# Gated mix of a spectral filter and a lookup of experts: last slices loaded once, one table along d, merged twiddle tables, one more late row buffer

## The chip, the core and the metric

The kernel runs on one core of one Trainium2 chip. The metric is the device time in microseconds (us) of one execution; several executions give a median. A profile is one further execution, recorded by the hardware profiler. Engines are called PE (matmuls), DVE (vector), ACT (scalar), POOL and SP (here used to issue transfers).

## The reference

x has 2048 rows (s) of 576 columns (d). Two results are mixed row by row with a gate.

```python
def A(x, w_r, w_i):                      # spectral filter
    X = rfft2(x, axes=(-2, -1)) * (w_r + 1j * w_i)
    return irfft2(X, s=(2048, 576), axes=(-2, -1))

def B(x, w_q, k1, k2, u, v):             # 32 heads, 64 x 64 experts, the best one
    q = einsum("nd,dhc->nhc", x, w_q)    # c: 2 x 128
    i1 = argmax(q[..., :128] @ k1.T); i2 = argmax(q[..., 128:] @ k2.T)
    e = i1 * 64 + i2                     # one row of u and of v per head
    g = softmax over the single best     # = 1
    return einsum("nhk,nhk,nhkd->nd", g, gelu(einsum("nd,nhkd->nhk", x, u[e])), v[e])

g = sigmoid((x * gate_w).sum(-1))
out = g * A + (1 - g) * B
```

## The kernel before

The 2048 rows are 16 tiles of 128. A small planner (`Plan`) holds the whole program: each helper (`dv`, `ac`, `ld`, `plan`) records a job with its engine, an assumed duration, a due time `at` and its buffers, which come from rings of a given size. `Plan.order` then lists the jobs by their due times, as their inputs and free buffers allow, and the loop at the end of `tile_kernel` writes each engine's instructions out in this order, chained so that no engine departs from it. The due times of the parts of A are multiples of the constant `FPACE`. A ring whose name is in `plan.late` opens only when the last job on a buffer of the score stage has ended; at that point (`switch`) the pools of the score stage are closed and new ones open in their place.

**Score stage.** The products of w_q and the keys are formed for one chunk of four heads at a time (`build_m`, 8 chunks): the 576 columns are cut into five slices i of 128, the last of which holds only 64, and carried twice. `load_wq` (L352) brings 512 KB for each chunk and slice on SP; 8 matmuls with the keys kT make 512 columns in PSUM; ACT (L396) copies these as the rounded high part `mh`, DVE (L397) subtracts it to get the low part `ml`. x comes transposed in blocks of 512 rows (`load_x`, L358): ACT (L361) makes its high part, DVE (L362) its low part. `scores` multiplies x and the products in high and low parts: three matmuls for each of the slices 0 to 3 (hi x hi, hi x lo, lo x hi) and two for the last slice, in which both copies of the 64 columns are used so that one matmul does two of these products. DVE takes the maximum of each 64 (L427), ACT the sign of the difference (L435), and a few small steps on ACT and DVE (L446 to L455) give the index. With mh and ml in rings of 8, chunk c+1 is built while chunk c is scored.

**Groups.** A group is a tile and a chunk, four heads. POOL issues a gather (L487) of 128 rows of u and v, joined to 1152 columns, into a buffer of the ring `uv` (12) or, late, `uv2`. DVE forms the product with x and sums it (L496), ACT the gelu (L500), DVE the factors a (L501). Then either DVE adds the four rows of v (L512, L514), or, for about half of the groups of tiles 10 to 15 and some others (`is_d`), ACT makes four diagonal matrices (L524) and PE multiplies with them (16 passes), and the PSUM result is copied or added (L538, L540). Groups of the tiles 0 to 9 run during the score stage, those of tiles 10 to 15 after it.

**The transform.** After the score stage `fold` splits each tile into sums and differences along d (DVE L649 to L651, ACT L648), multiplies with kr (five matmuls, PE) and ACT (L661, L662) spreads the result in `BT`. Then ten units follow: `f2` (six matmuls with the table `fi[0]`), `f4` (four matmuls with the twiddle table `t4`), `f5` (DVE L709 to L712, complex product with w), `f6` (matmuls with the table `t6`) and copies and sums back in `BT` (ACT L766, DVE L775 to L782). `turns` loads t4 and t6 for a unit on SP (L680, L681) and ACT (L682 to L684) makes the negated and doubled columns. After the last unit, `invert` takes each tile back: six matmuls with the table `fi[1]`, ACT L819, four matmuls with krb, ACT L830 and L831 with the gate as scale. `mix` (DVE L835) adds the part of B and stores the tile (SP). The kr table, the late tiles of x (L366), `fi[0]` (L638), the gate row (L639), `fi[1]` (L640) and krb (L641) are loaded by SP, in the written-out order; an SP load that waits for its buffer holds up those behind it.

The matmuls have one line, L313, that of the helper `mm`.

Of the kernel before, what the change touches and what calls it, by code (L numbers as in the profile page):

```python
# [19 lines left out]
P = 128  # L20
D = 576
# [11 lines left out]
def _tables():  # L33
# [19 lines left out]
    fwd = np.stack([  # L53
        rows(np.cos, np.arange(0, 128)), rows(np.cos, np.arange(128, 256)), ct,
        -rows(np.sin, np.arange(0, 128)), -rows(np.sin, np.arange(128, 256)), -st,
    ])
    ck = np.full(DF, 2.0)
    ck[0] = ck[-1] = 1.0
    ck /= S * D

    def irows(fn, ks):
        return fn(2 * np.pi * np.outer(ks, k) / D) * ck[ks][:, None]

    ct = z.copy()
    ct[:33] = irows(np.cos, np.arange(256, 289))
    st = z.copy()
    st[64:96] = irows(np.sin, np.arange(256, 288))
    inv = np.stack([
        irows(np.cos, np.arange(0, 128)), irows(np.cos, np.arange(128, 256)), ct,
        irows(np.sin, np.arange(0, 128)), irows(np.sin, np.arange(128, 256)), st,  # L70
# [12 lines left out]
        "t_fi": c(np.concatenate([fwd, inv]).transpose(1, 0, 2)),  # L83
        "t_f4": c(f4),
        "t_f6": c(f6),
# [167 lines left out]
def tile_kernel(ctx, tc, xn, xT, wqT, kT, wri, uv, gw, t_kr, t_fi, t_f4, t_f6, t_io, out):  # L253
# [84 lines left out]
    gate = pp.tile([P, NT], F32, tag="gate", name="gate")  # L338
    gone = pp.tile([P, NT], F32, tag="gone", name="gone")
# [12 lines left out]
    def load_wq(c, i, at, after=()):  # L352
        w = wq_t[c, i] = buf("uv", ROW, view=lambda x: x.rearrange("p a d -> p (a d)")[:, : 8 * P].rearrange("p (g e) -> p g e", g=8))
        ld(load(P * 4096, 4096), at, lambda: nc.sync.dma_start(w.ap, wqT[c, i]), [w], after=after)

    def load_x(b, i, at, at2):
        st = buf("uv", ROW, view=lambda x: x[:, 0, :512])
        ld(load(P * 2048, 2048), at, lambda: nc.sync.dma_start(st.ap, xT[:, i, b * 512 : b * 512 + 512]), [st])  # L358
        hi = xts[i if i < 4 else 8][b]
        lo, r = (xts[4 + i][b], 0) if i < 4 else (hi, 64)  # L360
        ac(act(512), at2, lambda: actv(hi.ap, st.ap, AF.Copy), [hi], [st])  # L361
        dv(dve(512), at2, lambda: vt(lo.ap[r:], st.ap[r:], hi.ap[r:].bitcast(F32), ALU.subtract), [lo], [st, hi])  # L362
# [18 lines left out]
    def build_m(c, i, at, after=()):  # L381
        mh, ml = m_t[c, i] = [buf(n, [P, CW], F32R) for n in ("mh", "ml")]
        pm = psum()
        wq = wq_t[c, i]
        pv = lambda: pm.ap.rearrange("p a (g e) -> p (a g) e", e=128)

        def go():
            for g in range(8):
                half = g % 2
                mm(  # L390
                    pv()[:, g, :], wq.ap[:, g, :],
                    kTb.ap[:, half * 64 : half * 64 + 128], start=True, stop=True)
# [3 lines left out]
        ac(act(512), at, lambda: actv(v3(mh), pv()[:, :, :E], AF.Copy), [mh], [pm])  # L396
        dv(dve(512, True), at, lambda: vt(v3(ml), pv()[:, :, :E], v3(mh).bitcast(F32), ALU.subtract), [ml], [pm, mh])  # L397
# [4 lines left out]
    def scores(c, tp, at):  # L402
# [4 lines left out]
        def part(j, i):  # L407
# [5 lines left out]
            seq = [(x, mh), (x, ml)] + ([(xts[4 + i][b], mh)] if i < 4 else [])  # L413

            def go():
                for n, (xx, m) in enumerate(seq):
                    mm(ps.ap[:, j, :], xx.ap[:, tsl], m.ap, start=i == n == 0, stop=i == 4 and n == len(seq) - 1)

            use = {id(q): q for pair in seq for q in pair}
            return plan("PE", 0.23 * len(seq), at, go, [(ps, j)], list(use.values()))  # L420
# [211 lines left out]
    fi = [buf("fi0", [P, 6, DF]), buf("fi1", [P, 6, DF])]  # L632
# [5 lines left out]
    ld(load(P * 6936, 4096), T0 + 8, lambda: nc.sync.dma_start(fi[0].ap, t_fi[:, 0:6, :]), [fi[0]])  # L638
    ld(0.5, T0 + 15, lambda: nc.sync.dma_start(gw2.ap, gw.partition_broadcast(P)), [gw2])  # L639
    ld(load(P * 6936, 4096), T0 + 90, lambda: nc.sync.dma_start(fi[1].ap, t_fi[:, 6:12, :]), [fi[1]])  # L640
# [4 lines left out]
    def fold(t, at):  # L645
        x = xs[t]
        f = buf("f5", [P, ND * P])
        ac(0.17, at, lambda: actv(f.ap[:, 0:385:384], x.ap[:, 0:1].to_broadcast([P, 2]), AF.Copy), [(f, 0)], [x])  # L648
# [28 lines left out]
    def turns(k, at):  # L677
        t4 = buf("t4", [P, 3, P])
        t6 = buf("t6", [P, 5, P])
        ld(load(P * 1024, 1024), at - 8, lambda: nc.sync.dma_start(t4.ap[:, 0:2, :], t_f4[k]), [(t4, 0)])  # L680
        ld(load(P * 1024, 1024), at - 8, lambda: nc.sync.dma_start(t6.ap[:, 0:2, :], t_f6[k]), [(t6, 0)])  # L681
        ac(act(128), at - 2, lambda: actv(t4.ap[:, 2, :], t4.ap[:, 1, :], AF.Copy, scale=-1.0), [(t4, 1)], [(t4, 0)])  # L682
        ac(act(256), at - 2, lambda: actv(t6.ap[:, 2:5:2, :], t6.ap[:, 0:1, :].to_broadcast([P, 2, P]), AF.Copy), [(t6, 1)], [(t6, 0)])
        ac(act(128), at - 2, lambda: actv(t6.ap[:, 3, :], t6.ap[:, 1, :], AF.Copy, scale=-1.0), [(t6, 2)], [(t6, 0)])  # L684
        tabs[k] = t4, t6

    def f4(k2, X, at):
# [16 lines left out]
        return p, w, t6

    def f5(p, w, t6, at):
# [4 lines left out]
        dv(dve(DF), at, lambda: vt(a.ap[:, 0, :], a.ap[:, 0, :], b.ap[:, 1, :], ALU.subtract), [(a, 0)], [b])  # L711
        dv(dve(DF), at, lambda: vt(a.ap[:, 1, :], a.ap[:, 1, :], b.ap[:, 0, :], ALU.add), [(a, 1)], [b])  # L712
        return a, t6

    def f6(k2, zb, t6, at):
        pt = psum()
        u, v = (0, 3) if k2 <= 8 else (2, 1)

        def go():
            z, T = zb.ap, t6.ap  # L720
# [9 lines left out]
        plan("PE", 4 * pe(256) + 4 * pe(128), at, go, [pt], [(zb, 0), (zb, 1), (t6, 0), (t6, 1), (t6, 2)])  # L730
# [10 lines left out]
    def unit_front(k2, at):  # L741
# [8 lines left out]
        ac(act(DF), at, lambda: actv(sr.ap[:, 0, :], psn.ap[:, 1, :DF], AF.Copy, scale=-1.0), [(sr, 0), sr], [psn])  # L750
        ac(act(DF), at, lambda: actv(sr.ap[:, 1, :], psn.ap[:, 0, :DF], AF.Copy), [(sr, 1), sr], [psn])
# [4 lines left out]
    def unit_back(z, at):  # L756
# [19 lines left out]
        dv(dve(256, True), at, lambda: vt(tslot(qs, 0), tm()[:, 1], mainv(pb)[:, 1], ALU.subtract), [(BT, "q", qs, 0)], src + [s_])  # L776
        dv(dve(256, True), at, lambda: vt(tslot(qs, 1), mainv(pb)[:, 0], tm()[:, 0], ALU.subtract), [(BT, "q", qs, 1)], src + [s_])
# [3 lines left out]
        dv(dve(128, True), at, lambda: vt(BT.ap[0:33, 2, :, qs], ta.ap[64:97, 512:], pb.ap[64:97, 1, :P], ALU.subtract), [s_], src)  # L781
        dv(dve(128, True), at, lambda: vt(BT.ap[64:96, 2, :, qs], pb.ap[0:32, 1, :P], ta.ap[0:32, 512:], ALU.subtract), [s_], src)  # L782
# [13 lines left out]
    def close_gates(at):  # L796
# [7 lines left out]
        dv(0.1, at, lambda: nc.vector.tensor_scalar(gone, gate, -1.0, 1.0, op0=ALU.mult, op1=ALU.add), ["gone"], ["gate"])  # L804

    gas = {}

    def invert(t, at):
        p = psum()

        def go():
            for r in range(2):
                for m, i in enumerate((3 * r, 3 * r + 1, 2)):
                    mm(p.ap[:, r, :DF], BT.ap[:, i, t * 8 : t * 8 + 8, :].rearrange("p j q -> p (j q)"),
                       fi[1].ap[:, 3 * r + m, :], start=m == 0, stop=m == 2)

        plan("PE", 6 * pe(DF), at, go, [p], [fi[1]] + every)
# [11 lines left out]
        g = gate[:, t : t + 1]  # L829
        ac(act(DF), at + 3, lambda: actv(ga.ap[:, :DF], p9.ap[:, 0, :DF], AF.Copy, scale=g), [(ga, 0)], [p9, "gate"])  # L830
        ac(act(DF), at + 3, lambda: actv(ga.ap[:, 575:288:-1], p9.ap[:, 1, 1:288], AF.Copy, scale=g), [(ga, 1)], [p9, "gate"])  # L831
# [98 lines left out]
```

## Time and profile before

| | before |
|---|---|
| median of 3 runs | 1009.44 us (1008.35 to 1010.46) |
| the profiled execution | 1001.24 us |
| span in its profile | 999.5 us |
| mean granted PE clock | 0.965 |
| PE busy | 904.4 us (90%) |
| DVE busy | 916.7 us (92%) |
| ACT busy | 514.6 us (51%) |
| POOL busy | 574.4 us (57%) |
| moved | 348.39 MB, 349 GB/s |

The span runs from the first to the last instruction of the core; the profiled execution's own time is 1.7 us longer. The profiled execution was shorter than the median of the timed ones; sums are made against it. In the profile a row names the line, engine, operation and tile names; an arrow to the left (`<-`) in brackets names what ended an idle time. A matmul of f32 operands shows two records (passes).

### The profile page before, as it was taken

To read this page: it belongs to the slowest core of one execution; us is meant where nothing else is said; L and a number is where in the kernel's file an instruction comes from. 1 tells how busy PE (TensorE), PEld (TensorE's weight loads), DVE (VectorE), ACT (ScalarE), POOL (GpSimd) and SP (SyncE) were. 2 spreads that over 40 slices of the span, in tenths; PEclk is the share of its full clock that TensorE was granted. 3 is DMA by queue.
4 is the path that set the end of the run, shared out by engine and by line. 5 is a ranking of instruction groups with operands and counts; after the bars stand their busy time and mean duration, and the time that the engine had idled before them with its cause. 6 is when DMAs were issued, how large, how long until landed. Compare 5 with 4: busy or idle time off the path is not lost. (4 is left out here: it accounts for less than half of the span.)

```text
span 999.5 us, 14406 instructions
## 1 busy us (share of the span) xinstructions
PE 904.4 (90%) x4208; PEld 735.8 (74%) x4208; DVE 916.7 (92%) x2255; ACT 514.6 (51%) x1877; POOL 574.4 (57%) x516
## 2 busy tenths in 40 slices
PE   8997999999999999999998990777999998899993
PEld 7885888878877888887877880665777776677762
DVE  3996999999999999999999999999999999977776
ACT  3874676676666576676666664522212222233331
POOL 0354656565656565755657566476655565676662
PEclk9997999999999999999999996889999999899998
DMA  9987999998989999998999799889999999999994
GB/s 336 336 286 301 349 361 367 358 352 305 392 309 361 371 344 332 395 345 328 386 360 330 291 394 378 340 312 389 394 357 351 357 353 321 349 390 414 398 359 192
DMA packets 93246, 348.39 MB, mean 349 GB/s; under 512 B 10480, under 2 KB 13296, under 8 KB 93168
## 3 DMA queue, kind: packets, MB, share of 16 engines
q0 software_dynamic: 73728, 302.02, 80.9%
q1 hardware_dynamic: 19440, 45.45, 12.3%
q8 instruction: 34, 0.56, 0.2%
q14 instruction: 44, 0.36, 0.1%
HBM read 342.71 MB, written 4.72 MB: 348 GB/s over the span
## 5 line engine op out<-in xcount | busy, mean ns | idle before, releaser
L487 POOL DMA_INDIRECT uv<-uv,ei x512 | 574.2, 1121 | 406.2 <-PE p L313 133.3
L313 PE MATMUL p<-mh,xt 128*128 128x512 f32 x1152 | 383.3, 402 | 9.1 <-ACT sg L435 7.3
L435 ACT ACTIVATE sg<-p,mx 128x64 bf16<-128x64 f32 x1024 | 225.8, 352 | 78.1 <-DVE mx L427 55.7
L514 DVE SCALAR_TENSOR_TENSOR xn<-uv,a,xn 128x576 f32<-128x576 f32 x322 | 262.0, 814 | 1.5
L313 PEld LDWEIGHTS p<-mh,xt 128*128 128x128 f32 x1152 | 218.4, 190 | 59.5 <-ACT sg L435 7.7
L313 PE MATMUL p<-ml,xt 128*128 128x512 f32 x640 | 253.2, 396 | 0.0
L496 DVE SCALAR_TENSOR_TENSOR uv<-uv,xn 128x576 f32<-128x576 f32 x320 | 236.3, 749 | 8.7 <-DMA uv<-uv,ei 6.8
L313 PE MATMUL p<-uv,dg 128*128 128x288 f32 x720 | 194.0, 425 | 29.3 <-ACT dg L524 22.5
L313 PEld LDWEIGHTS p<-uv,dg 128*128 128x128 f32 x720 | 140.8, 199 | 77.9 <-ACT dg L524 29.3
L496 DVE SCALAR_TENSOR_TENSOR uv<-uv,xl 128x576 f32<-128x576 f32 x192 | 141.5, 751 | 0.2
L313 PEld LDWEIGHTS p<-ml,xt 128*128 128x128 f32 x640 | 121.6, 190 | 26.6
L500 ACT ACTIVATE b<-z 128x4 f32<-128x4 f32 x128 | 26.4, 206 | 204.9 <-DVE uv L496 171.4
L313 PE MATMUL p<-fi,bt 128*128 128x289 f32 x384 | 97.7, 408 | 4.4 <-DVE t L710 3.0
L313 PEld LDWEIGHTS p<-fi,bt 128*128 128x128 f32 x384 | 83.5, 242 | 16.5 <-issue 3.7
L313 PEld LDWEIGHTS p<-kT,uv 128*128 128x128 f32 x640 | 77.8, 195 | 7.9 <-issue 4.8
L313 PE MATMUL p<-kT,uv 128*128 128x128 f32 x640 | 78.5, 279 | 5.0 <-DMA uv<-wqT 5.0
L427 DVE TENSOR_REDUCE mx<-p 128x16 f32<-128x1024 f32 x64 | 77.5, 1211 | 3.2 <-PE p L313 3.0
L313 PE MATMUL p<-t,t 128*128 128x289 f32 (+2 forms) x384 | 73.8, 362 | 5.9 <-issue 3.4
L446 ACT ACTIVATE sg<-sg 128x256 bf16<-128x256 bf16 x192 | 72.3, 427 | 1.2
L313 PEld LDWEIGHTS p<-t,t 128*128 128x128 f32 (+1 forms) x384 | 54.1, 165 | 23.9 <-issue 10.7
L524 ACT ACTIVATE dg<-ident,a 128x128 f32<-128x128 f32 x180 | 57.6, 393 | 17.7 <-DVE a L501 14.8
L313 PE MATMUL p<-kr,f 128*128 128x128 f32 x160 | 23.0, 301 | 31.5 <-ACT f L648 26.8
(86 smaller groups left out, 612.1 us busy)
## 6 DMA issues: line engine op xcount, KB each, us to landing
uv<-wqT SPq DMA_DIRECT2D x40, 512.0 KB
uv<-uv,ei POOLq DMA_INDIRECT x512
uv<-xT SPq DMA_DIRECT2D x20, 256.0 KB
w<-wri SPq DMA_DIRECT2D x16, 289.0 KB
out<-xn SPq DMA_DIRECT2D x16, 288.0 KB
xn<-xn SPq DMA_DIRECT2D x10, 288.0 KB
t<-t_f SPq DMA_DIRECT2D x18, 128.0 KB
fi<-t_fi SPq DMA_DIRECT2D x2, 867.0 KB
```

Source lines behind the costliest of these rows:

```text
L313: after("PE", nc.tensor.matmul(*args, **kw))
L427: dv(dve(1024, True), at, lambda: nc.vector.tensor_reduce(mv.ap[:, 2 * tp : 2 * tp + 2, :], ps.ap.rearrange("p a (g e) -> p a g e", e=E), ...
L435: on("ACT", actv(sg.ap[:, j, g, :], ps.ap[:, j, g * E : g * E + E], AF.Sign, bias=mv.ap[:, 2 * tp + j, g : g + 1], scale=-1.0))
L446: ac(act(256), at, lambda b=b: actv(s2()[:, :, b * Q : b * Q + Q], s2()[:, :, b * Q : b * Q + Q], AF.Copy, bias=b / 4), [sg], [])
L487: on("POOL", nc.gpsimd.indirect_dma_start(out=g.ap.rearrange("p a d -> p (a d)"), out_offset=None, in_=uv, in_offset=bass.IndirectOffsetOn ...
L496: dv(0.68, at, lambda k=k, g=rows[k]: stt(g.ap[:, 0, :], g.ap[:, 0, :], 1.0, x.ap, op0=ALU.mult, op1=ALU.mult, accum_out=z.ap[:, k : k + 1 ...
L500: ac(0.18, at - 9, lambda: actv(b.ap, z.ap, AF.Gelu_apprx_tanh), [b], zk, table="gelu")
L514: dv(0.73, at, lambda v=v, s=s: stt(y.ap, v(), s(), y.ap, op0=ALU.mult, op1=ALU.add), [y], [(rows[k], 1), a])
L524: ac(0.3, at - 9, lambda k=k, dg=dg: actv(dg.ap, ident, AF.Copy, scale=a.ap[:, k : k + 1]), [dg], [a, "ident"])
```

## The change

Seven things are changed.

- `load_wq` and `build_m`: the last slice of wq is loaded with its 64 columns once (256 KB). The 8 matmuls give 64 rows; ACT copies the high part twice, to the partitions 0 to 63 and 64 to 127; DVE writes the low part of 64 partitions.
- `load_x`: the last slice of x is loaded with 64 rows; its low part is written to partitions 64 to 127 as before. In `scores` the (hi, lo) matmul of the last slice uses 64 partitions.
- Blocks 2 and 3 of x come in one load each slice (512 KB), and block 3 is converted at the due time of block 2, where it was loaded and converted later.
- One table along d: `fi` is used by f2 and invert. What differed between the two tables is put elsewhere: the sign in additions and subtractions that swap their operands, the halved first row in `fold` (scale 2), the factor 2/(S D) in a scaled gate `gsc` (one DVE instruction in `close_gates`). `fi` is in the pool, and at the due time, that the following diff shows.
- t4 and t6 become one table `tw`: nine loads of 256 KB instead of 18 of 128 KB.
- The late ring `uv2` has 2 buffers instead of 1.
- `FPACE` is 1.4 instead of 1.7.

```diff
 def load_wq(c, i, at, after=()):
+    e = P if i < 4 else E
...
+    ld(load(P * e * 32, e * 32), at, lambda: nc.sync.dma_start(w.ap, wqT[c, i] if i < 4 else wq5[c]), [w], after=after)
 def load_x(b, i, at, at2, n=1):
...
+    ld(load(h * n * 2048, n * 2048), at, lambda: nc.sync.dma_start(st.ap[:h], src()), [st])
+    for m in range(n):
...
+        ac(act(512), at2, lambda hi=hi, cut=cut: actv(hi.ap[:h], cut(), AF.Copy), [hi], [st])
+        dv(dve(512), at2, lambda hi=hi, lo=lo, cut=cut: vt(lo.ap[r : r + h], cut(), hi.ap[:h].bitcast(F32), ALU.subtract), [lo], [st, hi])
 def build_m(c, i, at, after=()):
...
-    ac(act(512), at, lambda: actv(v3(mh), pv()[:, :, :E], AF.Copy), [mh], [pm])
+    for r in range(0, P, h):
+        ac(act(512), at, lambda r=r: actv(v3(mh)[r : r + h], pv()[:h, :, :E], AF.Copy), [(mh, r)], [pm])
...
 for i in range(ND):
-    load_x(2, i, 15, 24)
+    load_x(2, i, 15, 24, 2)
...
-for i in range(ND):
-    load_x(3, i, 34, when(3))
...
-        ("t2", "ip", NT2), ("bt", "ip", 1), ("fi1", "ip", 1), ("krb", "ip", 1),
+        ("t2", "ip", NT2), ("bt", "ip", 1), ("fi", "ip", 1), ("krb", "ip", 1),
         ("uv2", "x2", NG2), ("xl", "x2", NT - NE), ("gr", "x2", 1),
-        ("f5", "fp", 2), ("kr", "fp", 1), ("fi0", "fp", 1), ("t4", "fp", 2), ("t6", "fp", 2), ("w", "fp", 2)):
+        ("f5", "fp", 2), ("kr", "fp", 1), ("tw", "fp", 2), ("w", "fp", 2)):
...
-ld(load(P * 6936, 4096), T0 + 8, lambda: nc.sync.dma_start(fi[0].ap, t_fi[:, 0:6, :]), [fi[0]])
+ld(load(P * 6936, 4096), T0 + 8, lambda: nc.sync.dma_start(fi.ap, t_fi), [fi])
-ld(load(P * 6936, 4096), T0 + 90, lambda: nc.sync.dma_start(fi[1].ap, t_fi[:, 6:12, :]), [fi[1]])
...
+    tw = tabs[k] = buf("tw", [P, 8, P])
+    ld(load(P * 2048, 2048), at - 8, lambda: nc.sync.dma_start(tw.ap[:, 1:5, :], t_tw[k]), [(tw, 0)])
...
+    dv(0.1, at, lambda: nc.vector.tensor_scalar(gsc, gate, 2.0 / (S * D), None, op0=ALU.mult), ["gsc"], ["gate"])
...
-NG2 = 1
+NG2 = 2
-FPACE = 1.7
+FPACE = 1.4
```

More of the change, by code (lines that the diff above doesn't have):

```diff
@@ L47, in _tables @@
     z = np.zeros((P, DF))
+    c0 = rows(np.cos, np.arange(0, 128))
+    c0[0] *= 0.5
     ct = z.copy()
@@ L52, in _tables @@
     st[64:96] = rows(np.sin, np.arange(256, 288))
[L53 to L70, printed above, removed]
+    fi = np.stack([
+        c0, rows(np.cos, np.arange(128, 256)), ct,
+        rows(np.sin, np.arange(0, 128)), rows(np.sin, np.arange(128, 256)), st,
     ])
@@ L82, in _tables @@
         "t_kr": c(np.stack([kr, krb], axis=1)),
-        "t_fi": c(np.concatenate([fwd, inv]).transpose(1, 0, 2)),
-        "t_f4": c(f4),
-        "t_f6": c(f6),
+        "t_fi": c(fi.transpose(1, 0, 2)),
+        "t_tw": c(np.concatenate([f4[:, :, ::-1], f6], 2)),
     }
@@ L252, in tile_kernel @@
 @with_exitstack
-def tile_kernel(ctx, tc, xn, xT, wqT, kT, wri, uv, gw, t_kr, t_fi, t_f4, t_f6, t_io, out):
+def tile_kernel(ctx, tc, xn, xT, x5, wqT, wq5, kT, wri, uv, gw, t_kr, t_fi, t_tw, t_io, out):
     nc = tc.nc
@@ L338, in tile_kernel @@
     gate = pp.tile([P, NT], F32, tag="gate", name="gate")
+    gsc = pp.tile([P, NT], F32, tag="gsc", name="gsc")
     gone = pp.tile([P, NT], F32, tag="gone", name="gone")
@@ L352, in load_wq, with load_x @@
     def load_wq(c, i, at, after=()):
[L353 to L362, printed above, removed]
+        e = P if i < 4 else E
+        w = wq_t[c, i] = buf("uv", ROW, view=lambda x: x.rearrange("p a d -> p (a d)")[:, : 8 * e].rearrange("p (g e) -> p g e", g=8))
+        ld(load(P * e * 32, e * 32), at, lambda: nc.sync.dma_start(w.ap, wqT[c, i] if i < 4 else wq5[c]), [w], after=after)
+    def load_x(b, i, at, at2, n=1):
+        st = buf("uv", ROW, view=lambda x: x.rearrange("p a d -> p (a d)")[:, : n * 512])
+        h = P if i < 4 else E
+        src = lambda: xT[:, i, b * 512 : (b + n) * 512] if i < 4 else x5[:, b * 512 : (b + n) * 512]
+        ld(load(h * n * 2048, n * 2048), at, lambda: nc.sync.dma_start(st.ap[:h], src()), [st])
+        for m in range(n):
+            hi = xts[i if i < 4 else 8][b + m]
+            lo, r = (xts[4 + i][b + m], 0) if i < 4 else (hi, E)
+            cut = lambda m=m: st.ap[:h, m * 512 : m * 512 + 512]
+            ac(act(512), at2, lambda hi=hi, cut=cut: actv(hi.ap[:h], cut(), AF.Copy), [hi], [st])
+            dv(dve(512), at2, lambda hi=hi, lo=lo, cut=cut: vt(lo.ap[r : r + h], cut(), hi.ap[:h].bitcast(F32), ALU.subtract), [lo], [st, hi])
     def load_xn(t, tag, at):
@@ L384, in build_m @@
         wq = wq_t[c, i]
+        h = P if i < 4 else E
         pv = lambda: pm.ap.rearrange("p a (g e) -> p (a g) e", e=128)
@@ L412, in part @@
             x = xts[i if i < 4 else 8][b]
-            seq = [(x, mh), (x, ml)] + ([(xts[4 + i][b], mh)] if i < 4 else [])
+            h = P if i < 4 else E
+            seq = [(x, mh, P), (x, ml, h)] + ([(xts[4 + i][b], mh, P)] if i < 4 else [])
             def go():
[L416 to L420, printed above, removed]
+                for n, (xx, m, k) in enumerate(seq):
+                    mm(ps.ap[:, j, :], xx.ap[:k, tsl], m.ap[:k], start=i == n == 0, stop=i == 4 and n == len(seq) - 1)
+            use = [x, (ml, 0)] + [(mh, r) for r in range(0, P, h)] + ([xts[4 + i][b]] if i < 4 else [])
+            return plan("PE", 0.23 * len(seq), at, go, [(ps, j)], use)
         seq = [(j, i) for i in range(ND) for j in range(2)] if tp in (0, 7) else [(j, i) for j in range(2) for i in range(ND)]
@@ L669, in go @@
                 for n, i in enumerate(((0, 1, 2), (3, 4, 2))[r]):
-                    mm(p.ap[:, r, :DF], BT.ap[:, i, :, q], fi[0].ap[:, 3 * r + n, :], start=n == 0, stop=n == 2)
-        plan("PE", 6 * pe(DF), at, go, [p], [fi[0], (BT, "q", q)] + [(BT, "in", t, i) for t in range(NT) for i in range(2)])
+                    mm(p.ap[:, r, :DF], BT.ap[:, i, :, q], fi.ap[:, 3 * r + n, :], start=n == 0, stop=n == 2)
+        plan("PE", 6 * pe(DF), at, go, [p], [fi, (BT, "q", q)] + [(BT, "in", t, i) for t in range(NT) for i in range(2)])
         return p
@@ L677, in turns @@
     def turns(k, at):
[L678 to L685, printed above, removed]
+        tw = tabs[k] = buf("tw", [P, 8, P])
+        ld(load(P * 2048, 2048), at - 8, lambda: nc.sync.dma_start(tw.ap[:, 1:5, :], t_tw[k]), [(tw, 0)])
+        ac(act(128), at - 2, lambda: actv(tw.ap[:, 0, :], tw.ap[:, 1, :], AF.Copy, scale=-1.0), [(tw, 1)], [(tw, 0)])
+        ac(act(256), at - 2, lambda: actv(tw.ap[:, 5:8:2, :], tw.ap[:, 3:4, :].to_broadcast([P, 2, P]), AF.Copy), [(tw, 2)], [(tw, 0)])
+        ac(act(128), at - 2, lambda: actv(tw.ap[:, 6, :], tw.ap[:, 4, :], AF.Copy, scale=-1.0), [(tw, 3)], [(tw, 0)])
     def f4(k2, X, at):
@@ L691, in f4, with f5 @@
             turns(k2, at)
-        t4, t6 = tabs[min(k2, 16 - k2)]
-        a, b = (1, 2) if k2 <= 8 else (2, 1)
+        tw = tabs[min(k2, 16 - k2)]
+        a, b = (0, 1) if k2 <= 8 else (1, 0)
         p = psum()
         def go():
-            T, x, o = t4.ap, X.ap, p.ap
-            mm(o[:, 0, :DF], T[:, 0, :], x[:, 0, :], start=True, stop=False)
+            T, x, o = tw.ap, X.ap, p.ap
+            mm(o[:, 0, :DF], T[:, 2, :], x[:, 0, :], start=True, stop=False)
             mm(o[:, 0, :DF], T[:, a, :], x[:, 1, :], start=False, stop=True)
-            mm(o[:, 1, :DF], T[:, 0, :], x[:, 1, :], start=True, stop=False)
+            mm(o[:, 1, :DF], T[:, 2, :], x[:, 1, :], start=True, stop=False)
             mm(o[:, 1, :DF], T[:, b, :], x[:, 0, :], start=False, stop=True)
-        plan("PE", 4 * pe(DF), at, go, [p], [X, (t4, 0), (t4, 1)])
-        return p, w, t6
-    def f5(p, w, t6, at):
+        plan("PE", 4 * pe(DF), at, go, [p], [X, (tw, 0), (tw, 1)])
+        return p, w, tw
+    def f5(p, w, tw, at):
         a = t2()
@@ L824, in go9 @@
                 mm(p9.ap[:, r, :DF], krb.ap[:, 0, :], pq.ap[:, 0, :], start=True, stop=False)
-                mm(p9.ap[:, r, :DF], krb.ap[:, 1 - r, :], pq.ap[:, 1, :], start=False, stop=True)
+                mm(p9.ap[:, r, :DF], krb.ap[:, r, :], pq.ap[:, 1, :], start=False, stop=True)
         plan("PE", 4 * pe(DF), at + 3, go9, [p9], [(krb, 0), (krb, 1), pq])
         ga = gas[t] = t2((P, D)) if t in E_T else buf("xl", [P, D])
-        g = gate[:, t : t + 1]
-        ac(act(DF), at + 3, lambda: actv(ga.ap[:, :DF], p9.ap[:, 0, :DF], AF.Copy, scale=g), [(ga, 0)], [p9, "gate"])
-        ac(act(DF), at + 3, lambda: actv(ga.ap[:, 575:288:-1], p9.ap[:, 1, 1:288], AF.Copy, scale=g), [(ga, 1)], [p9, "gate"])
+        g = gsc[:, t : t + 1]
+        ac(act(DF), at + 3, lambda: actv(ga.ap[:, :DF], p9.ap[:, 0, :DF], AF.Copy, scale=g), [(ga, 0)], [p9, "gsc"])
+        ac(act(DF), at + 3, lambda: actv(ga.ap[:, 575:288:-1], p9.ap[:, 1, 1:288], AF.Copy, scale=g), [(ga, 1)], [p9, "gsc"])
     def mix(t, at):
@@ L888, in is_d @@
     return t % 2 == 0 if t >= NE else t in (1, 4, 8) and c < NCH - 1
-_INS = ["xn", "xT", "wqT", "kT", "wri", "uv", "gw", "t_kr", "t_fi", "t_f4", "t_f6", "t_io"]
+_INS = ["xn", "xT", "x5", "wqT", "wq5", "kT", "wri", "uv", "gw", "t_kr", "t_fi", "t_tw", "t_io"]
 def _layout(A_x, A_w_r, A_w_i, B_w_q, B_k1, B_k2, B_u, B_v, gate_w):
```

45 lines of the change are left out of this document (22 added, 23 removed).

## The prediction

> **What bounds the kernel now.** I read the span cut into stretches first: busy us of each engine per stretch, then the granted clock, the DMA share and GB/s.
>
> ```profile
> 0.00:25.00 25.00, 20.04 (x120) 18.10 (x121) 8.85 (x13) 8.98 (x18) 0.20 (x4) 1.00 0.94 336
> 25.00:50.00 25.00, 25.00 (x127) 20.99 (x126) 22.88 (x58) 21.33 (x72) 8.46 (x8) 1.00 0.94 335
> 100.00:200.00 100.00, 99.67 (x487) 82.76 (x486) 98.83 (x250) 66.98 (x257) 61.20 (x54) 1.00 0.95 358
> 500.00:600.00 100.00, 96.36 (x431) 78.08 (x430) 97.53 (x243) 66.13 (x259) 61.17 (x54) 0.98 0.92 344
> 600.00:650.00 50.00, 19.73 (x128) 17.41 (x127) 49.73 (x127) 26.81 (x102) 28.16 (x24) 0.73 0.94 360
> 627.00:860.00 233.00, 202.98 (x947) 166.32 (x948) 225.46 (x552) 65.56 (x212) 136.29 (x125) 0.95 0.96 353
> 860.00:1000.00 140.00, 121.86 (x495) 92.83 (x493) 103.23 (x240) 42.49 (x114) 80.00 (x72) 0.97 0.90 347
> ```
>
> Columns are length, PE, weight loads, DVE, ACT, POOL. In the score stage (to about 601 us) PE and DVE are both full and the transfers nearly so. From 600 to 860 DVE is full (225.46 of 233) and PE is not. From 860 to the end PE leads (121.86 of 140) and DVE idles 37 us. Which waits stand behind that is in the lists of waits: DVE over the span, DVE from 850 on, PE from 595 to 660, PE from 0 to 100.
>
> ```profile
> DVE uv L496 <- DMA uv<-uv,ei: 6.8, 10, 1.2
> ...
> DVE xn L835 <- ACT t L831: 7.7, 7, 2.0
> ...
> DVE xn L835 <- ACT xn L538: 4.2, 1, 4.2
> ```
> ```profile
> PE p L313 <- ACT f L648: 26.8, 1, 26.8
> ...
> PE p L313 <- ACT sg L435: 7.3, 1, 7.3
> PE p L313 <- DMA uv<-wqT: 5.0, 2, 4.8
> ```
>
> Transfers are busy, but in the whole run DVE waited 6.8 us for gathered rows and PE 5.0 us for wq, nearly all of it at the start. PE's 26.8 us before the first fold is time in which DVE works off the groups of the score stage. The end is seen in PE's and DVE's timelines and in the chain of work that ended last:
>
> ```profile
> 859.49 2.46 PE L313 MATMUL p<-t,t 128*128 128x256 f32 x16
> ...
> 862.68 107.72 PE p L313 x440
> ...
> 975.12 4.15 PE L313 MATMUL p<-uv,dg 128*128 128x288 f32 x16 [1.77 <-ACT dg L524]
> 984.64 5.84 PE L313 MATMUL p<-uv,dg 128*128 128x288 f32 x16 [5.38 <-ACT dg L524]
> ```
> ```profile
> 991.19 0.82 DVE L835 SCALAR_TENSOR_TENSOR xn<-xn,gone,xl 128x576 f32<-128x576 f32 x1 [4.24 <-ACT xn L538]
> ...
> 992.12 3.38 DVE L514 SCALAR_TENSOR_TENSOR xn<-uv,a,xn 128x576 f32<-128x576 f32 x4
> 995.54 0.82 DVE L835 SCALAR_TENSOR_TENSOR xn<-xn,gone,xl 128x576 f32<-128x576 f32 x1
> ```
> ```profile
> L712 DVE TENSOR_TENSOR t<-t,t x16: 446/454/458, 679.4 to 857.9; 128x289 f32<-128x289 f32 x16
> ...
> L649 DVE TENSOR_TENSOR f<-xn x10: 483/485/494, 627.6 to 643.0; 128x319 f32<-128x319 f32 x10
> ```
>
> So there are three pieces: the score stage, 230.8 us from the first fold (627.6) to the end of the last f5 (857.9 + 0.45), bound by DVE, and 136.9 us from the last f6 (859.49) to DVE's end (995.54 + 0.82 = 996.4), nearly all packed PE work. A time changes where one of these three changes.
>
> **The change part by part.** *Bytes.* The last slice of wq loses 256 KB in each of 8 chunks (2.10 MB), that of x 0.52 MB, the second table along d 0.89 MB: 3.51 MB of these 348.39.
>
> ```profile
> DMA packets 93246, 348.39 MB, mean 349 GB/s; under 512 B 10480, under 2 KB 13296, under 8 KB 93168
> ...
> 4.80 3.75 PE L313 MATMUL p<-kT,uv 128*128 128x128 f32 x16 [4.80 <-DMA uv<-wqT]
> ```
>
> If transfers set the pace everywhere this is 3.51 MB / 349 GB/s = 10.1 us; if they are hidden it is nothing. At the start, PE waits for the first slice of wq until 4.80, which is not shortened; afterwards it is busy 20.04 of the first 25 us, so at most 25 - 4.8 - 20.04 = 0.2 us is left to gain there, and in the next 25 it is busy all the time. I take 0.2 for it. From the 6.8 us for gathers I take 1.0, nearer to nothing than to all, because only 1% of the bytes goes. The term is 1.2, its ends are 0 and 10.1; it lies near 0 because the waits that it could shorten are short.
>
> The profile moved 358 GB/s from 100 to 200 us. [...]
>
> The last slice of x now fills 64 partitions, not 128. [...] No run here shows a load of 64 partitions yet.
>
> *More ACT and DVE work.* Per chunk, the last slice gets a second high copy: 8 x 0.613 = 4.9 us on ACT, busy 66 to 67 of each 100 us. DVE gets one more small instruction (gsc).
>
> ```profile
> L396 ACT ACTIVATE mh<-p 128x512 fp32r<-128x512 f32 x40 | 24.5, 613 | 19.4 <-remote 9.2 <-PE p L313 7.7 <-issue 2.5
> ...
> L804 DVE TENSOR_SCALAR gone<-gate 128x16 f32<-128x16 f32 x1 | 0.4, 391 | 0.0
> ```
> ```profile
> 83.23 0.60 ACT L396 ACTIVATE mh<-p 128x512 fp32r<-128x512 f32 x1 [4.08 <-remote]
> ...
> 88.50 0.79 PE L313 MATMUL p<-mh,xt 128*128 128x512 f32 x1 [7.28 <-ACT sg L435]
> ```
>
> ACT's third of idle time hides the copies, except at the first chunk boundary, where PE stalled 7.28 us for ACT's sign row, which stood behind a high copy that itself waited 4.08. Nothing there is removed; one copy more adds 0.6 if it comes in the stall, else 0. I take 0 and keep 0.6 (if that cover is gone everywhere, 4.9). gsc is 0.4, and lies on DVE before the last f5. The signs that move between tables, additions and subtractions change no duration; the score passes keep their number, and weights of fewer columns don't shorten a pass:
>
> ```profile
> L313 PE MATMUL p<-kT,uv 128*128 128x128 f32 x640 | 78.5, 279 | 5.0 <-DMA uv<-wqT 5.0
> ...
> L313 PE MATMUL p<-t,t 128*33 128x128 f32 x128 | 10.2, 279 | 0.0
> ```
>
> *One table, one twiddle table.* Twiddle bytes stay, 18 loads become 9. But the single table along d takes the place of the second, and that load waited on SP:
>
> ```profile
> 602.59 0.91 SPq L638 DMA_DIRECT2D fi<-t_fi  x1
> ...
> 627.77 0.33 SPq L640 DMA_DIRECT2D fi<-t_fi  x1
> ...
> 666.28 2.08 PE L313 MATMUL p<-fi,bt 128*128 128x289 f32 x7 [0.69 <-ACT bt L661]
> ...
> 641.45 0.29 ACT L682 ACTIVATE t<-t 128x128 f32<-128x128 f32 x1
> ```
>
> In the changed order the fi load has the old second table's place in memory, freed by the last score step, so its issue moves from 602.6 to about 627.7. The gate row, the first w, tw, w, tw and krb, issued at 603 to 611 before, are queued behind it on SP. The first use of fi is at 666.28: 38 us of cover for 0.89 MB, which at a third of 360 GB/s takes 7.4 us. The first ACT copy of a twiddle is at 641.45: cover 13.7 us for fi, gate, w and tw, 1.74 MB, 4.8 us at all of 360 GB/s and 14.5 at a third of it. I cost it at 0; at a third it is 0.8 late, and ACT's evictions of the folds stand behind it. Later tw loads wait for an f6 instead of an f4, but the f6 of two units before, a unit (about 22 us) ahead of its need: 0.
>
> *Order of the late stage (FPACE, one more gather buffer).* POOL's order is unchanged. DVE has 1150 instructions before the first fold in both programs. From there to the last f5 it has 128 products (L496) and 70 sums (L514, L512) instead of 123 and 66; after the last f5, 76 and 40 instead of 81 and 44.
>
> ```profile
> 645.62 0.73 DVE xn L514
> ...
> 649.42 2.04 DVE uv L496 x6
> ```
>
> The chain gives three products with their accumulator reads in 2.04 us, so 0.68 each, and 0.73 for a sum; four sums in a row took 3.38, 0.85 each. That is 5 x 0.68 + 4 x 0.8 = 6.6 us, with gsc about 6.9: DVE is full there, so the last f5 ends 6.9 us later. In the tail PE has the same work after the start of the last f6 in both: 240 matmuls of 2 passes and the f6, by 107.72 us for 440 passes 117.5 + 2.5 = 120 us. What differs is the last piece. Before, both of the last two diagonal groups (16 passes) came behind the last krb, and DVE still had their products to do: 136.9. Changed, one group comes behind the last krb: 116 us to there, then ACT's scale and evictions 1.4, the last products 0.75, gelu, a and diagonals 0.9, the group on PE 5.8, its copy 0.7, mix 0.8, four sums 3.4, mix 0.8: 130.6. The tail is 6.3 shorter. The sum of both is +0.6.
>
> The 14th gather buffer lets gathers run further ahead, but DVE's waits for gathers from 600 on are 0: it takes none away.
>
> Sum: -0.2 - 1.0 + 0.6 (gsc in it) = -0.6. The profiled execution took 1001.24 us, 1.7 around its span of 999.5; -0.6 gives 1000.6. The median of the timed runs, 1009.44, is 1.0082 times the profiled time, so the forecast is 1000.6 x 1.0082 = 1008.8 us.
>
> **The rivals.** (1) *Transfers bind all along.* For it: 0.92 to 0.96 DMA share through 600 us; against it: 6.8 us of waits on gathers. 1001.24 - 10.1 = 991.1, that is 999.3.
>
> (2) *The tail closes up.* DVE idles 37 us after 860 behind ACT (L831, L538). If the earlier group work spreads ACT's rows, a quarter of it (9 us) goes: 992.2, that is 1000.4. Against it: PE's 120 us stay.
>
> (3) *Slower: the last f5 moves and the tail does not shrink.* The last f5 is 6.9 later; if the last diagonals wait for gelu and ACT as before (5.4 and 1.8), the tail stays at 136.9: 1001.24 + 6.9 - 1.8 = 1006.3, that is 1014.6. It decides when the tail shrinks by less than 3 of its 6.3. For it: PE's end in the tail follows the last f6, and the waits sit between ACT and PE, where the written-out order does not say how long they are.
>
> (4) *Slower: the late loads or the first boundary.* Loads behind SP's wait come after their cover, or the boundary stall of 7.3 us comes a second time: +7.3 - 0.6 gives 1007.9, that is 1016.2; with (3) too, 1021.
>
> (5) *The bytes are saved and no time with them*, late stage even: 1009.4.
>
> **How the numbers follow.** Forecast 0.32 (own range 1005 to 1012); (1) 0.13; (2) 0.17; (3) 0.23; (4) 0.09; (5) 0.06. A measurement of this kernel can tell about 0.2%, 2 us, from no change. Faster: 0.12 from the edge of the forecast's case, (1) and (2): 0.42. Same: 0.12 from its middle and (5): 0.18. Slower: 0.08 from its other edge, (3) and (4): 0.40. Cases of both signs hold much, so the range reaches from below (1) by its own 3 us, 996, to (3) with half of (4), 1018; left out are (1) with (2), and (3) with (4).
>
> **What would show it.** Right: the last L712 ends some 237 us after the first L649, and DVE's end follows the last f6 by about 131 us, with one wait of PE on L524 instead of two. DVE's wait for gathers falls by about a us and PE stays full to 600. Wrong: a score stage shorter by 5 us or more (then rival 1); an ACT wait on tw or a PE wait on fi between 640 and 670 (rival 4); a tail of 135 us or more (rival 3), or of under 125 (rival 2).

## The result and the profile after

| | before | changed |
|---|---|---|
| median of 4 runs | 1008.89 us (1006.11 to 1010.46) | 1042.02 us (1040.16 to 1044.80) |
| ratio | | 1.0334, 95% interval 1.0301 to 1.0367 |
| the profiled execution | 1001.24 us, span 999.5 | 1044.80 us, span 1042.9 |
| PE busy | 904.4 us | 960.4 us |
| DVE busy | 916.7 us | 916.6 us |
| moved | 348.39 MB | 344.88 MB |
| first fold / end of the last f5 / DVE's end | 627.6 / 858.4 / 996.4 | 664.0 / 907.2 / 1039.9 |

The changed kernel is 3.3% slower; 1008.8 us was forecast and 996 to 1018 given as the range. The two profiles lie 43.5 us apart, 10 more than the medians, because the profile of before was its quickest execution here (1001.24 us against a median of 1008.89) and that of the changed kernel the slowest of its four; they serve to place the loss, not to size it.

Three quarters and more of the loss are in the score stage, which the prediction had left nearly as it was (1.2 us less for bytes): the first fold comes 36.4 us later. The stretches of the changed kernel (length, PE, weight loads, DVE, ACT, POOL, clock, DMA share, GB/s):

```profile
0.00:25.00 25.00, 19.55 (x113) 17.09 (x114) 8.49 (x13) 8.30 (x13) 0.20 (x4) 1.00 0.95 328
...
100.00:200.00 100.00, 100.00 (x449) 74.29 (x448) 89.05 (x222) 62.29 (x243) 56.77 (x51) 1.00 0.89 331
...
500.00:600.00 100.00, 99.97 (x431) 73.12 (x432) 94.01 (x231) 63.47 (x252) 56.04 (x49) 1.00 0.90 332
600.00:650.00 50.00, 42.83 (x166) 30.10 (x164) 46.65 (x122) 28.76 (x108) 30.74 (x28) 0.95 0.85 308
```

Before, DVE worked 98.8 of the 100 us from 100 on; now it works 89.1 and PE has no gap. But PE's records in that stretch have fallen from 487 to 449: it is full and does less. Matmul for matmul nothing was added (4208 in both), so single passes must hold PE longer. The groups of the score passes by shape (out, in, partitions x columns of the weights, shape, count | busy, mean ns), the first line before, the others changed:

```profile
L313 PE MATMUL p<-ml,xt 128*128 128x512 f32 x640 | 253.2, 396 | 0.0
```
```profile
L299 PE MATMUL p<-ml,xt 128*128 128x512 f32 x512 | 201.4, 393 | 0.0
...
L299 PE MATMUL p<-ml,xt 64*128 64x512 f32 x128 | 63.8, 498 | 0.0
...
L299 PEld LDWEIGHTS p<-ml,xt 64*128 64x128 f32 x128 | 23.4, 183 | 44.6 <-issue 43.5 <-DVE lc L462 0.4 <-DVE xn L509 0.4
```

128 passes have the new form, over 64 partitions. The passes overlap in the records (below, 0.40 us long at starts 0.23 apart), so a mean tells little; what counts is their starts, in PE's timeline:

```profile
597.03 0.63 PE L299 MATMUL p<-mh,xt 128*128 128x512 f32 x2
597.50 0.40 PE L299 MATMUL p<-ml,xt 128*128 128x512 f32 x1
597.73 0.63 PE L299 MATMUL p<-mh,xt 128*128 128x512 f32 x2
598.29 0.50 PE L299 MATMUL p<-ml,xt 64*128 64x512 f32 x1
598.72 0.50 PE L299 MATMUL p<-mh,xt 128*128 128x512 f32 x1
599.06 0.39 PE L299 MATMUL p<-ml,xt 128*128 128x512 f32 x1
599.29 0.62 PE L299 MATMUL p<-mh,xt 128*128 128x512 f32 x2
```

Ordinary passes start 0.23 us apart (597.03 to 597.73, three passes, 0.70). From 597.73 to 599.06 there are four, and they take 1.33 instead of 0.93: the pass over 64 partitions starts 0.10 late, the one after it 0.20, the next 0.11. That is 0.40 us for this one, an estimated 51 us for 128. The timeline of the weight loads shows what is lost:

```profile
597.50 0.42 PEld L299 LDWEIGHTS p<-mh,xt 128*128 128x128 f32 x2
598.29 0.18 PEld L299 LDWEIGHTS p<-ml,xt 64*128 64x128 f32 x1 [0.36 <-issue]
598.72 0.19 PEld L299 LDWEIGHTS p<-mh,xt 128*128 128x128 f32 x1 [0.25 <-issue]
598.83 0.19 PEld L299 LDWEIGHTS p<-ml,xt 128*128 128x128 f32 x1
```

The two loads from 597.50 to 597.92 follow each other with no idle time marked and lie under the passes that run from 597.03 on; the load for 64 partitions begins 0.36 us after the last load ended, and the one at the way back again 0.25 after. DVE waited for little before, and now waits for PE. Its two longest waits from 100 to 600 us before, then those of the changed kernel:

```profile
DVE uv L496 <- DMA uv<-uv,ei: 5.4, 8, 1.2
DVE xn L540 <- PE p L313: 1.5, 2, 1.3
```
```profile
DVE xn L535 <- PE p L299: 12.5, 10, 2.3
DVE uv L491 <- DMA uv<-uv,ei: 9.6, 14, 1.7
DVE mx L422 <- remote: 7.1, 3, 2.7
DVE mx L422 <- PE p L299: 4.4, 7, 2.1
```

(The figures are us in total, times and the longest. L540 before and L535 now add the diagonal groups' PSUM, L422 takes the maximum of the scores.)

### The profile page after: what moved, and what is told of

Read it like the earlier page. It is cut to its first block, busy times and chain, and to the rows that moved or that the text cites. A ratio compares the mean times of both kernels' runs of the same rounds, so it can differ in the third digit from the quotient of the medians.

```text
span 1042.9 us, 14370 instructions
## 1 busy us (share of the span) xinstructions
PE 960.4 (92%) x4208; PEld 730.0 (70%) x4208; DVE 916.6 (88%) x2256; ACT 521.0 (50%) x1885; POOL 577.5 (55%) x516
## 2 busy tenths in 40 slices
DMA packets 90894, 344.88 MB, mean 331 GB/s; under 512 B 10240, under 2 KB 10752, under 8 KB 90816
## 4 chain that ended last, share of the span: by engine, by line
PE 68%; DVE 22%; DMA 4%; issue 3%; ACT 1%; POOL 1%; another core or an unknown queue 1%; SPq 0%; POOLq 0%; DVEq 0%; ACTq 0%
PE p L299 68%; DVE uv L491 7%; DVE xn L509 7%; DMA uv<-uv,ei 4%; DVE mx L422 1%; DVE t L699 1%; DVE t L700 1%; POOL uv L482 1%; DVE sg L443 1%; DVE bt L765 0%; DVE p L369 0%; DMA uv<-wqT 0%; DVE t L701 0%; DVE f L641 0%
## 5 line engine op out<-in xcount | busy, mean ns | idle before, releaser
L299 PE MATMUL p<-mh,xt 128*128 128x512 f32 x1152 | 390.7, 409 | 2.4 <-issue 2.4
L299 PE MATMUL p<-ml,xt 128*128 128x512 f32 (+1 forms) x640 | 265.2, 414 | 0.0
L299 PE MATMUL p<-uv,dg 128*128 128x288 f32 x720 | 194.7, 426 | 13.7 <-ACT b L495 5.8
L299 PEld LDWEIGHTS p<-ml,xt 128*128 128x128 f32 (+1 forms) x640 | 120.1, 188 | 62.5 <-issue 43.5
L299 PE MATMUL p<-fi,bt 128*128 128x289 f32 x384 | 101.5, 419 | 9.1 <-DVE t L700 6.7
L422 DVE TENSOR_REDUCE mx<-p 128x16 f32<-128x1024 f32 x64 | 78.0, 1219 | 20.1 <-PE p L299 9.3
L299 PE MATMUL p<-kT,uv 128*128 128x128 f32 (+1 forms) x640 | 82.0, 284 | 5.5 <-DMA uv<-wqT 5.5
L299 PEld LDWEIGHTS p<-kT,uv 128*128 128x128 f32 (+1 forms) x640 | 75.5, 185 | 13.0 <-issue 10.8
L390 ACT ACTIVATE mh<-p 128x512 fp32r<-128x512 f32 (+1 forms) x48 | 28.8, 600 | 44.6 <-PE p L299 33.9
L299 PE MATMUL p<-tw,t 128*128 128x256 f32 (+1 forms) x256 | 42.0, 344 | 8.0 <-DVE t L701 6.8
```

What stands on the lines that cost most here:

```text
L299: after("PE", nc.tensor.matmul(*args, **kw))
L390: ac(act(512), at, lambda r=r: actv(v3(mh)[r : r + h], pv()[:h, :, :E], AF.Copy), [(mh, r)], [pm])
L422: dv(dve(1024, True), at, lambda: nc.vector.tensor_reduce(mv.ap[:, 2 * tp : 2 * tp + 2, :], ps.ap.rearrange("p a (g e) -> p a g e", e=E), ...
```

## The experiments

Theory S is that the change between 64 and 128 partitions makes the time; rival L that the late stage, the queue on SP and ACT's extra copies do. All the experiments ran where the kernel before takes 991 to 992 us, so ratios to it are compared, not times.

**The pass over 64 partitions alone, in the kernel before.**

```diff
-    mm(ps.ap[:, j, :], xx.ap[:, tsl], m.ap, ...)
+    k = E if i == 4 and n == 1 else P
+    mm(ps.ap[:, j, :], xx.ap[:k, tsl], m.ap[:k], ...)
```

> The kernel before, with one thing changed: the second matmul of the last slice (x, ml) uses 64 partitions instead of 128 (it leaves out the product of the two low parts). Theory S, a pass over 64 partitions between passes over 128 holds PE 0.4 us longer (in the trace of after four passes around one take 1.33 us, 597.73 to 599.06, where four take 0.93): 128 x 0.4 = 51 us more PE work, less the some 10 us that PE has idle in the score stage, so 1042 to 1050 us. Rival L, the late stage (order, tables behind SP's wait) and the second high copy on ACT make the time: 1009 us, no change.

Measured: 1022.59 us, ratio 1.0348 (1.0313 to 1.0382). One index makes all of the loss. Its groups are those of the changed kernel:

```profile
L313 PE MATMUL p<-ml,xt 128*128 128x512 f32 x512 | 201.3, 393 | 0.0
...
L313 PE MATMUL p<-ml,xt 64*128 64x512 f32 x128 | 63.8, 498 | 0.0
```

Nearly all of the loss lies ahead of the first fold, which starts at 651.0 us where it starts at 619.9 in the profile of the kernel before that is shown further down:

```profile
L650 DVE TENSOR_TENSOR f<-xn x10: 480/484/489, 651.0 to 666.1; 128x319 f32<-128x319 f32 x10
```

The size fits the ratio rather than the times that S gave, which were for the slower chip: 31.6 us of 51, where a cover of some 10 was expected. L is refuted for the loss as a whole.

**The changed kernel with all score passes over 128 partitions**, in two ways: wq's last slice loaded twice as before, or loaded once and its low part written twice.

```diff
 # e2_wq_twice (and _layout concatenates the slice with itself)
-    e = P if i < 4 else E
+    e = P
-    h = P if i < 4 else E          # build_m, scores
+    h = P
```
```diff
 # e2d_ml_copy
-    dv(dve(512, True), at, lambda: vt(v3(ml)[:h], pv()[:h, :, :E], v3(mh)[:h]..., ALU.subtract), [(ml, 0)], [pm, (mh, 0)])
+    for r in range(0, P, h):
+        dv(dve(512, True), at, lambda r=r: vt(v3(ml)[r : r + h], pv()[:h, :, :E], v3(mh)[:h]..., ALU.subtract), [(ml, r)], [pm, (mh, 0)])
-    seq = [(x, mh, P), (x, ml, h)] + ...
+    seq = [(x, mh, P), (x, ml, P)] + ...
```

> The changed kernel with the last slice of wq loaded twice again, so that build_m and the scores run over 128 partitions; all else is as changed (x, one table, tw, NG2 2, FPACE 1.4). Theory S: the 33 us go, 1004 to 1014 us. Rival L: it stays near 1042 us, at least over 1030.

> The changed kernel, wq's last slice loaded once, but DVE writes the low part a second time to partitions 64 to 127, so that all score passes run over 128 partitions. Theory S: as with the slice loaded twice, plus at most 8 x 0.68 = 5.4 us of DVE and less 2.1 MB: 1003 to 1019 us. Rival L, with ACT's second high copy still there: 1042 us or more.

Measured: 988.75 us, ratio 0.9982 (0.9955 to 1.0010), and 992.94 us, ratio 1.0027 (1.0005 to 1.0049). The loss is gone in both. The second keeps every byte that the change saves and ACT's second high copy, and it keeps the weights of 64 columns in `build_m`; none of these cost the 33 us. In its profile the first fold comes at 627.9 us, 8.0 later than the 619.9 of the kernel before. The 8 x 0.68 = 5.4 us that it adds on DVE (0.676 us for each low part over 64 partitions in the changed kernel's profile, L391) and an estimated 2.4 us that weights of 64 columns cost PE (last section) would make this up, but that is argued. Its median is 4.2 us above the first variant's; run again, the first came out at 1.0013, so that the two can't be told apart.

**The two passes over 64 partitions of a step beside each other.**

```diff
+    def tail():                      # one job for the last slice of both tiles
+        for m, k in ((mh, P), (ml, E)):
+            for j in range(2):
+                mm(ps.ap[:, j, :], xs_[j].ap[:k, cut[j]], m.ap[:k], start=False, stop=k == E)
-    js = [part(j, i) for j, i in seq]          # i in range(ND)
+    js = [part(j, i) for j, i in seq] + [tail()]   # i in range(4)
```

> The changed kernel with the two passes over 64 partitions of a step next to each other (the last slice of both tiles: both high passes, then both low passes). Theory S, cost at the change between 64 and 128 partitions: half of the changes go, about 26 of the 51 us of PE, so 1016 to 1025 us. Variant S2, a pass over 64 partitions is itself slower whatever stands beside it: 1042 us. Rival L: 1042 us.

Measured: 1006.56 us, ratio 1.0181 (1.0153 to 1.0208), about half of the loss. PE's timeline:

```profile
299.78 0.74 PE L299 MATMUL p<-ml,xt 64*128 64x512 f32 x2
300.44 0.50 PE L299 MATMUL p<-mh,xt 128*128 128x512 f32 x1
300.78 0.39 PE L299 MATMUL p<-ml,xt 128*128 128x512 f32 x1
...
305.91 0.86 PE L299 MATMUL p<-mh,xt 128*128 128x512 f32 x3
306.70 0.73 PE L299 MATMUL p<-ml,xt 64*128 64x512 f32 x2
307.37 3.94 PE L299 MATMUL p<-kT,uv 128*128 128x128 f32 x32
```

Two adjoining passes take 0.66 us to the next start (299.78 to 300.44), where one alone took 0.43 (598.29 to 598.72): the second costs the ordinary 0.23. So the price hangs on the change there and back, not on the number of passes; S2, a pass slow in itself, falls. The next experiment agrees: it has 64 narrow passes, not 128, and also changes there and back 64 times, and it costs nearly the same (14.7 us above the kernel before, against 15.6 here).

**Half of the chunks.**

```diff
-    k = E if i == 4 and n == 1 else P
+    k = E if i == 4 and n == 1 and c % 2 == 0 else P
```

> The kernel before, with the low matmul of the last slice over 64 partitions in the even chunks alone (64 passes of 128; the product of the two low parts is left out there). PE gets 25.6 us more work. If PE's idle time in the score stage is a reserve that must be used up first (with all 128 passes 51 us of work cost some 32, so a reserve of about 19): ratio to before about 1.006. If the cost is proportional to the passes: half of 3.5%, 1.017.

Measured: 1006.48 us, ratio 1.0146 (1.0118 to 1.0173). It is the proportional answer, or nearly; the reserve of 19 us for the whole stage is refuted. In the first profile of before PE's idle time is spread over the chunks (22 us in the first 600, no wait longer than 7.3), and a chunk seems unable to use what another leaves. That last point is argued, not shown.

**What the rest of the change is worth.** The variant with wq's last slice twice was run with FPACE 1.7, then also with one buffer in `uv2`, then again with FPACE 1.4, and with 1.2 and 1.0 (one constant each).

> The changed kernel with wq's last slice twice (as e2_wq_twice, ratio 0.998) and FPACE 1.7 again. If the pace of the transform brings what is gained after the score stage (first fold to the end 364.3 us in e2_wq_twice against 368.7 in the profile before): about 4 us slower than e2_wq_twice, ratio 1.002. If it comes from elsewhere or is chance, as my prediction's sum of +0.6 has it: ratio 0.996 to 1.000.

> As e4_f17, with one late gather buffer less (13 again). DVE waits for no gather after 600 us in the profile before, so it should be the same as e4_f17 within 0.2%; if the buffer matters for the late stage, slower by 2 us or more.

> The kernel of e2_wq_twice once more (the changed kernel with wq's last slice twice, so that all score passes run over 128 partitions). If all the rest of the change is worth a little: ratio 0.995 to 0.999, as in the first run (0.998). If that was chance and the rest is worth nothing, as my prediction's sum of -0.6 us has it: 0.999 to 1.001.

> e6_wq_twice_again with FPACE 1.2. If a faster pace of the transform takes idle time from DVE's tail (129.7 us from the last f5 to the end, of which DVE works about 98): 2 us or more faster than e6_wq_twice_again. If it only moves group work from the tail to ahead of the last f5, where DVE is full: the same within 0.2%.

> As e7_f12 with FPACE 1.0. By the first reason faster again by 2 us; by the second the same, or slower by some us because the units then come sooner than DVE can serve them and PE waits for f5.

| | FPACE | gather buffers late (12 and those of `uv2`) | ratio to before |
|---|---|---|---|
| e2_wq_twice | 1.4 | 14 | 0.9982 (0.9955 to 1.0010) |
| e6_wq_twice_again | 1.4 | 14 | 1.0013 (0.9993 to 1.0034) |
| e4_f17 | 1.7 | 14 | 1.0015 (0.9995 to 1.0034) |
| e5_f17_n1 | 1.7 | 13 | 1.0009 (0.9991 to 1.0027) |
| e7_f12 | 1.2 | 14 | 1.0098 (1.0076 to 1.0121) |
| e8_f10 | 1.0 | 14 | 1.0216 (1.0198 to 1.0235) |

The rest is worth nothing that can be measured, and neither the buffer nor FPACE 1.4 against 1.7 shows a difference in time. The buffer does change the order, and FPACE 1.4 does not: from the first fold to the last f5 it takes 234.1 us in e4_f17 (FPACE 1.7, 14 buffers) and 234.0 in e6_wq_twice_again (1.4), but 227.3 in e5_f17_n1 (13 buffers), about as before (228.2). My expectations for the faster paces failed: against e6_wq_twice_again they are slower by 8 and 20 us. For 1.2 that was in neither of the two reasons; for 1.0 the second reason allowed some us, from PE waiting for f5. In both, the last f5 comes earlier and the tail is longer by more: first fold to the last f5 228.2 and 217.5 us, from there to the end 143.7 and 165.1, against 234.0 and 131.5 with 1.4. For 1.0 DVE's list of waits from 850 us on names the reason for the tail:

```profile
DVE uv L491 <- DMA uv<-uv,ei: 33.9, 32, 3.0
DVE a L496 <- ACT b L495: 8.3, 17, 1.9
DVE xn L826 <- ACT xn L533: 3.9, 1, 3.9
```

The group work put off behind the units meets its own gathers: in e6_wq_twice_again DVE waits for none there. The first fold of e8_f10 comes 5.6 us later besides, for which I have no cause. With 1.2, eight products and four sums more stand behind the last f5, and the longest wait is another, DVE's mix for ACT (14.7 us, L826 for L822, against 11.4 in e6_wq_twice_again); what makes the tail 12 us longer is not shown.

A run of the kernel before gave a profile on a chip as quick as these:

> The kernel before once more, unchanged, for a profile on the chip of these runs. Each theory expects a ratio of 1; of use is where its first fold, last f5 and end lie on this chip (627.6, 858.4 and 996.4 us in the first profile).

It took 989.42 us. First the first row of the folds, the last row of f5 and the late mixes there, then the same three in e6_wq_twice_again (start of the first and of the last instruction):

```profile
L649 DVE TENSOR_TENSOR f<-xn x10: 484/485/489, 619.9 to 635.0; 128x319 f32<-128x319 f32 x10
...
L712 DVE TENSOR_TENSOR t<-t,t x16: 445/454/460, 671.1 to 847.6; 128x289 f32<-128x289 f32 x16
...
L835 DVE SCALAR_TENSOR_TENSOR xn<-xn,gone,xl x6: 815/819/820, 930.2 to 983.7; 128x576 f32<-128x576 f32 x6
```
```profile
L641 DVE TENSOR_TENSOR f<-xn x10: 480/485/492, 619.9 to 633.6; 128x319 f32<-128x319 f32 x10
...
L702 DVE TENSOR_TENSOR t<-t,t x16: 453/455/468, 679.0 to 853.4; 128x289 f32<-128x289 f32 x16
...
L826 DVE SCALAR_TENSOR_TENSOR xn<-xn,gone,xl x6: 814/818/868, 942.8 to 984.5; 128x576 f32<-128x576 f32 x6
```

The first fold starts at the same 619.9. From it the last f5 ends after 228.2 and 234.0 us, and the tail takes 136.5 and 131.5.

No version beats the kernel before: the best ratio, 0.9982, came out as 1.0013 when it was run again.

## Why the prediction was wrong

- **The step that failed** is in the part on ACT and DVE: "the score passes keep their number, and weights of fewer columns don't shorten a pass". It priced fewer columns in `build_m`, with a row of 33 columns, and never priced the other edit of the same slice, a score pass over 64 partitions. No row of before has a matmul over fewer than 128 partitions, so by its own method this was an operation to bound from both sides, and it was taken at 0 without a bound. The row of 33 columns was read by its mean of 279 ns alone. The loads of weights around it, in the profile of before, show that a change of shape costs PE time (PE's weight loads, before):

```profile
712.10 1.59 PEld L313 LDWEIGHTS p<-t,t 128*128 128x128 f32 x8 [0.20 <-issue]
714.03 0.37 PEld L313 LDWEIGHTS p<-t,t 128*33 128x33 f32 x8 [0.33 <-issue]
714.59 1.52 PEld L313 LDWEIGHTS p<-t,t 128*128 128x128 f32 x7 [0.20 <-issue]
```

  They stop for 0.33 us on entering the narrow shape and 0.20 on leaving it, and the first narrow pass starts 0.31 us after the pass ahead of it, where 0.22 is usual. This was no price for 64 partitions, but a sign that such a price was to be looked for. The runs put 0.40 us for each change there and back in its place, an estimated 51 us of PE work, of which some 32 reach the time. What in PE makes this price, no run shows. None of the five rivals contained it, so the range could not hold the time.
- **The bound** was read too narrowly. "PE and DVE are both full" was in the text, from 99.67 and 98.83 of 100 us, but PE's part was then used only for the start and the late stage. With PE busy for 577.7 of the first 600 us (96%) any addition to its 1792 score passes had little cover.
- **Bytes** (1.2 us of gain, at most 10.1): transfers do not bind. With all 3.51 MB saved and PE's passes whole, e2d_ml_copy is 0.3% above before, by its interval 0.5 to 4.9 us. Taking off all of the 5.4 us on DVE and the estimated 2.4 on PE that it adds would leave a gain of 7.3 us at most, so 10.1 is excluded; 1.2 can be neither shown nor excluded. The part of it that was to come from shorter waits for gathers did not show: from 100 to 600 us DVE waited 6.3 us for them in the second profile of before, 6.3 in e6_wq_twice_again and 5.9 in e2d_ml_copy. In the changed kernel, at a DMA share of 0.89, it was 9.6. Rival 1 fell. Nor were the 358 GB/s from 100 to 200 us the most that the kernel before moved: from 900 to 950 us it was 405. What a load into 64 partitions takes can be read in the list of transfers of e2_wq_twice (size, median us from issue to landing), where `x` is the last slice of x, into 64 partitions, and `xT` the others, into 128:

```profile
uv<-xT SPq DMA_DIRECT2D x8, 256.0 KB, 6.2
...
uv<-x SPq DMA_DIRECT2D x2, 128.0 KB, 7.3
```

  Half the rows did not make the load shorter: 7.3 us against 6.2. These are two loads, beside other traffic.
- **ACT's second copies**, costed at 0: right within what can be told, by e2d_ml_copy, which keeps them.
- **The late loads behind SP's wait**, costed at 0: right in the changed kernel, about a microsecond short where PE is whole. The shared table was issued when the last score step let it go, and the first twiddle copy came 14.4 us later, against a cover of 13.7 forecast:

```profile
664.13 0.33 SPq L631 DMA_DIRECT2D fi<-t_fi  x1
...
678.50 0.31 ACT L673 ACTIVATE tw<-tw 128x128 f32<-128x128 f32 x1
...
700.10 6.23 PE L299 MATMUL p<-fi,bt 128*128 128x289 f32 x24 [0.69 <-ACT bt L653]
```

  ACT waited for no table there; PE's first use of fi waited 0.69 for the fold's eviction, as before. In e6_wq_twice_again, where fi was issued at 620.01, ACT did wait, as in the prediction's slower case (0.8 late) and its sign for rival 4:

```profile
635.09 0.31 ACT L673 ACTIVATE tw<-tw 128x128 f32<-128x128 f32 x1 [0.98 <-DMA tw<-t_tw]
```

  No time is seen to hang on it: e5_f17_n1 has no such wait and a like ratio, 1.0009.
- **The late stage**, last f5 +6.9 and tail -6.3: right in kind and nearly in size. With PE whole (e6_wq_twice_again against the second profile of before) they are +5.8 and -5.0, the sum +0.8 where +0.6 stood. The prediction did not say which of its two edits moves the order; by e4_f17 and e5_f17_n1 it is the buffer. Rivals 2, 3 and 4 fell: they would be ratios of about 0.991, 1.005 and 1.007, and e6_wq_twice_again has 0.9993 to 1.0034. Rival 5, no change, can't be told from the sum of -0.6. In the changed kernel itself the stretch to the last f5 grew by 12.4 and the tail shrank by 5.2; of the 6.6 beyond the pure case a single stall holds 5.3 (DVE's L699, its releaser not named by the profile), and its cause stays open.

## What to carry to other kernels

When an edit narrows an operand, price both dimensions of each matmul that reads it: columns and partitions. A pass over 64 partitions between passes over 128 cost 0.40 us here, and the second of two adjoining ones no more than an ordinary pass (0.23), so pad it (here the whole loss went: ratios 0.9982 and 1.0027), or put such passes side by side (here about half of it: 1.0181). Read the starts of passes, not their mean durations. When an engine is at 96% of a stage, even if another one is called the bound, a few tenths of a microsecond per instruction are the first thing to look for; the saved bytes brought nothing here that could be measured, as DVE waited for gathers in only 5.4 of the 500 us from 100 on in the first profile of before.

## What the runs showed of the hardware

- A change of a matmul from 128 to 64 partitions and back cost 0.40 us of PE time (changed kernel, 597.73 to 599.06; fp32r, 512 columns, 0.23 us from start to start of ordinary passes): 0.10 and 0.20 on entering and leaving and 0.11 on the pass after. The second of two adjoining passes over 64 partitions cost 0.23 (e3_grouped, 0.66 for two against 0.43 for one).
- Weights of 64 columns over all 128 partitions show a price of the same kind, though their mean duration hides it (276 ns against 282). In e2d_ml_copy, `build_m` makes 16 such passes in a row for each chunk. The first starts 0.20 us after the pass ahead of it and the second 0.16 after the first, where 0.11 is usual; the first score pass behind them starts 0.20 us after the last, where it is 0.03 behind weights of 128 columns, and the one after it 0.34 later, where it is 0.31. That makes an estimated 0.3 us for each stretch, 2.4 us for the eight. PE's weight loads at the end of one stretch show the gap:

```profile
76.84 0.19 PEld L299 LDWEIGHTS p<-mh,xt 128*128 128x128 f32 x1 [0.17 <-issue]
```
